# Clustered attention and two feed-forward layers: moving the preparation of a pair of heads within its steps, and rewriting the first head's start

## The chip, the cores and the metric

The kernel runs on one core of one Trainium2 chip. A time is that of one execution on the device in microseconds (us), and smaller is better. The core has five engines with an instruction queue each: TensorE (PE in the profile, with its weight loads apart as PEld), VectorE (DVE), ScalarE (ACT), GpSimd (POOL) and SyncE (SP). SP, and here ACT too, issue DMA transfers. SBUF is the memory on the core; PSUM is the accumulator memory that TensorE writes, in banks.

## The reference

```python
def _attn_ref(q, k, v, centroids):          # 2 batches, 8 heads, 768 rows, 64 wide; 16 centroids a head
    q_n, k_n, c_n = each divided by its norm along the last axis
    q_assign = np.argmax(np.einsum('bhsd,hcd->bhsc', q_n, c_n), axis=-1)
    k_assign = np.argmax(np.einsum('bhsd,hcd->bhsc', k_n, c_n), axis=-1)
    mask = q_assign[:, :, :, None] == k_assign[:, :, None, :]
    scores = np.where(mask, q @ k.T / 8, -1e9)
    return softmax(scores) @ v

x = attention, laid out as 1536 tokens x 512
h = x @ w_in1;  x = softplus(h) @ w_out1                 # 512 -> 2048 -> 512
h = x @ w_in2;  out = (h * clip(h + 3, 0, 6) / 6) @ w_out2
```

A query sees only the keys whose nearest centroid is its own. The matmuls are done on operands split into a rounded part (`hi`) and a rest (`lo`).

## The kernel before

**Stage one, attention.** Two heads form a pair, and there are 8 pairs (two batches of four). A pair takes 12 steps, six blocks of 128 queries for each head, so there are 96 steps. All of stage one is in program order on each engine: the loop at L769 to L792 calls the parts of a step one after the other, for steps -3 to 102, and works several steps ahead. In one turn of the loop these stand: `expo` (ACT, L410: exp with the row sums), `row_max` (DVE, L402: `nm`), `flip` twice (PE transposes `t`, L424; ACT copies them to `pth`, L428; DVE makes the rest `ptl`, L429), `scores` (PE, L394: `s`), `weigh` (PE, L439: `pv`). After every third turn `gather` copies a finished block of `pv` to SBUF (`xs`; ACT, L452 and L454).

**Preparation of a pair.** Between these parts lie seven numbered places, and `at(step, place, function, ...)` hangs a piece of other work there. The table at L515 to L602 does so for the preparation of each later pair. For pair n, with o = 12n - 12: q and k are loaded and split into hi and lo (POOL, L257 to L268; for the first two pairs ACT and DVE); `p_sims` multiplies them by the centroids (PE, `psm`, L294); `p_sims_out` scales that into `sT` (ACT, L300, by `c_r`, one over the centroids' norms); `p_back` transposes it (PE, `pbk`, L307); `p_max` and `p_equal` find the nearest centroid (DVE, `mx` L316 and `eq` L322, both read `pbk` in PSUM); `p_rank` breaks ties (POOL, L329); `p_best` and `p_first` finish the one-hot (DVE, L334 and `oh` L339); `p_onehot` transposes it (PE, `po`, L347); `p_mask` makes the mask rows `mk` (ACT, L353). SP's DMAs then assemble the operands `Q` and `K` from the parts (`assemble`, L371 to L375, and `assemble_mask`, L383).

**One bank for four tiles.** `psm`, `pbk` and `po` of every pair but the first, and `pb`, the transposed row sums of a finished pair (`tot_flip`, PE, L469; ACT copies it to `rT`, L474), come from one pool of PSUM with one buffer:

```python
def bank(n, shape, dt, name):
    if n == 0: ...
    else:
        pl, tag = ps_p, "prep"
```

A tile of it is written only when the last reader of the one before has ended. `tot_flip` of pair n hangs in step 12n + 15, place 0, and that is within the preparation of pair n + 2; it is so for six pairs.

**The start.** SP's queue loads `cT` (the centroids transposed), q and k of the first pair in halves, and `c_sb` (the centroids by rows, four DMAs, L208). A chain of small DVE and ACT operations makes `c_r` of it (L689 to L702, `c_sq` first). The first head's `Q` and `K` come by five DMAs. Then follow the one-hot of the first head, the scores and the loop.

**Stage two, the layers.** 96 steps in a pipeline, each with `h` (PE, L157), the activation `hid_scalar` (for the first layer two softplus on ACT: `g` at L812, `ghi` at L813) and `y` (PE, L845 and L847). The first of them are mixed by the scheduler with the last steps of stage one, as are the conversions of weights (ACT L98 and L122, DVE L106 to L112, POOL or DVE L133, `val`, `pi`, `po`). Softplus and exp lie in different table sets of ScalarE, so a load of the table stands ahead of each change.

Of the kernel before, what the change touches and what calls it, by code (L numbers as in the profile page):

```python
# [8 lines left out]
F32 = mybir.dt.float32  # L9
# [3 lines left out]
AF = mybir.ActivationFunctionType  # L13
# [9 lines left out]
def cluster_attention_then_two_mlps(  # L23
# [13 lines left out]
    nc = tc.nc  # L37
# [17 lines left out]
    def f32(ap):  # L55
        return ap.bitcast(F32)
# [89 lines left out]
    ps_h = []  # L146
    hs = {}

    def phase_a(n, c):
# [11 lines left out]
    def attention():  # L161
        with ExitStack() as st, ExitStack() as st_ld, ExitStack() as st_ps:
# [252 lines left out]
            def flip(t, g):  # L415
                h, jj = t // JH, t % JH
                if jj == 0 and g == 0:
                    st_t[h] = tuple(ptp.tile([P, NJ, HALF], F32R, tag=u, name=u) for u in ("pth", "ptl"))
                pth, ptl = st_t[h]
                pr = st_p[t]  # L420
                pt = ps_t.tile([P, 512], F32, tag="t", name="t")
                for c in range(JH):
                    kt = g * JH + c
                    nc.tensor.transpose(pt[:, c * P:(c + 1) * P], pr[:, kt * P:(kt + 1) * P], ident)  # L424
                src = pt[:, :HALF].rearrange("p (c q) -> p c q", q=P)
                dh = pth[:, g * JH:(g + 1) * JH, jj * P:(jj + 1) * P]
# [88 lines left out]
            for n in range(NP):  # L515
                o = SL * n - SL
                if n > 1:
                    at(max(o + -15, 3), 6, load_qk, n, "q")
                    at(max(o + -11, 4), 6, load_qk, n, "k")
                    at(max(o + -10, 4), 5, p_centroids, n)  # L520
                    q0 = max(o + -11, 7)
                    at(q0, 1, p_split_hi, n, "q", 0)
                    at(q0, 2, p_split_lo, n, "q", 0)
                    at(o + -4, 1, p_split_hi, n, "q", 1)
                    at(o + -4, 2, p_split_lo, n, "q", 1)
                    at(o + -3, 5, p_split_hi, n, "k", 0)
                    at(o + -2, 1, p_split_lo, n, "k", 0)
                    at(o + -1, 1, p_split_hi, n, "k", 1)
                    at(o + -1, 2, p_split_lo, n, "k", 1)
                    at(o + 0, 4, p_sims, n, 0)  # L530
                    at(o + 0, 4, p_sims, n, 1)
                    at(o + 1, 1, p_sims, n, 2)
                    at(o + 1, 4, p_sims, n, 3)
# [4 lines left out]
                    at(o + 3, 4, p_rank, n)  # L538
                    at(o + 4, 6, p_best, n)
                    at(o + 5, 1, p_first, n)  # L540
                    at(o + 6, 4, p_onehot, n)
                    at(o + 6, 6, p_mask, n)
# [4 lines left out]
                    at(o + -3, 6, load_v, n)  # L547
                    at(o + 6, 5, p_values, n, 0)
                    at(o + 7, 4, p_values, n, 1)
                elif n:  # L550
                    at(0, 4, p_centroids, n)
                    at(0, 2, p_split_hi, n, "q", 0)
                    at(0, 2, p_split_lo, n, "q", 0)
                    at(0, 4, p_split_hi, n, "q", 1)
                    at(0, 4, p_split_lo, n, "q", 1)
                    at(1, 2, p_split_hi, n, "k", 0)
                    at(1, 2, p_split_lo, n, "k", 0)
                    at(1, 5, p_split_hi, n, "k", 1)
                    at(1, 5, p_split_lo, n, "k", 1)
                    at(2, 3, p_sims, n, 0)  # L560
                    at(2, 5, p_sims, n, 1)
                    at(3, 3, p_sims, n, 2)
                    at(3, 3, p_sims, n, 3)
                    at(3, 4, p_sims_out, n)
                    at(4, 3, p_back, n)
                    at(4, 6, p_max, n)
                    at(5, 1, p_equal, n)
                    at(5, 1, p_rank, n)
                    at(6, 0, p_best, n)
                    at(6, 0, p_first, n)  # L570
                    at(7, 3, p_onehot, n)
                    at(7, 3, p_mask, n)
                    at(6, 3, assemble, n, 0)
                    at(8, 2, assemble_mask, n, 0)
                    at(11, 3, assemble, n, 1)
                    at(11, 6, assemble_mask, n, 1)
                    at(1, 1, load_v, n)
                    at(7, 0, p_values, n, 0)
                    at(10, 3, p_values, n, 1)
                o += 2 * SL  # L580
                if n < NP - 1:
# [5 lines left out]
                    at(o + 10, 4, fin_scale, n, 1)  # L587
                    at(o + 12, 2, fin_hi, n, 0)
                    at(o + 14, 2, fin_hi, n, 1)
                    at(o + 16, 2, fin_lo, n, 0)  # L590
# [173 lines left out]
            place(1, 0, 1)  # L764
            assemble(0, 1)
            p_values(0, 0)
            fetch_w(0, 0)
# [107 lines left out]
    with tc.manual_schedule():  # L875
# [11 lines left out]
        for n in range(len(steps) + LAG):  # L887
# [18 lines left out]
            if t:  # L906
                hid_scalar(t)
            do(convert_rest, ci, engine=nc.vector)
# [55 lines left out]
```

## Time and profile before

| | us |
|---|---|
| time, median of 3 runs (lowest, highest) | 805.5 (804.8, 806.54) |
| the profiled execution | 804.36 |
| its span | 802.6 |

The mean granted clock is 0.998 in the profiled execution. Busy shares of the span, by engine: PE 96%, DVE 58%, ACT 52%, POOL 19%. The profile shows one execution. The waits list says for each instruction of an engine what ended its idle time; a timeline gives every instruction with its start, its length and, in brackets, the idle time of its engine ahead of it and what ended that; the table of windows gives busy time by engine in a stretch, with the clock that TensorE was granted. Line numbers are those of the kernel before; in the kernel after, the same code stands 3 to 18 lines lower.

### The profile page before, as it was taken

Reading aid. Unit: us, or ns where it says so; the run is one execution under the profiler, and the core shown is the slowest. Engines: PE = TensorE matmul, PEld = TensorE weight load, DVE = VectorE, ACT = ScalarE, POOL = GpSimd, SP = SyncE. Lnnn points to the kernel's source line nnn. Section 1 sums busy time; section 2 is a strip of 40 time slices with the busy share of each in tenths; the row PEclk is TensorE's granted clock in tenths of the full one; section 3 lists DMA queues with packets and bytes.
Section 4 is the critical chain, followed back from the end, with each engine's and each line's share of the span. In section 5 each row is a group of like instructions: output and inputs, shape, how many; then the busy total and the mean of one; then the engine's idle time right before and its main releaser. Section 6 shows DMA issues by size and latency. Waiting matters only on the chain.

```text
span 802.6 us, 10560 instructions
## 1 busy us (share of the span) xinstructions
PE 768.0 (96%) x3835; PEld 643.9 (80%) x3835; DVE 465.0 (58%) x793; ACT 415.8 (52%) x828; POOL 152.2 (19%) x223
## 2 busy tenths in 40 slices
PE   5899898998999899999999999999999999999998
PEld 5788887887878678888888888888888888888886
DVE  5998878778788699942111247779862322232222
ACT  3888788888889856633122234455542222232221
POOL 4466657566333300000000000000000000000000
PEclk9999999999999999999999999999999999999999
DMA  8866455474366092000000156550000100010001
GB/s 210 262 161 164 93 158 134 97 185 94 79 147 228 18 371 104 1 0 1 1 0 1 51 186 205 182 190 27 2 1 0 53 1 0 1 53 0 1 1 52
DMA packets 38180, 70.53 MB, mean 88 GB/s; under 512 B 4432, under 2 KB 22512, under 8 KB 38128
## 3 DMA queue, kind: packets, MB, share of 16 engines
q1 hardware_dynamic: 38128, 69.86, 30.3%
q8 instruction: 30, 0.49, 0.3%
q14 instruction: 22, 0.18, 0.1%
HBM read 46.30 MB, written 3.19 MB: 62 GB/s over the span
## 4 chain that ended last, share of the span: by engine, by line
PE 81%; ACT 6%; DVE 6%; DMA 3%; issue 2%; SPq 1%; ACTq 0%; DVEq 0%
PE h L157 32%; PE y L847 16%; PE y L845 16%; PE s L394 5%; PE t L424 5%; PE pv L439 5%; DMA K<-hik 2%; ACT pth L428 2%; ACT pr L410 2%; PE psm L294 2%; DVE nm L402 1%; DVE ptl L429 1%; SPq L373 1%; ACT mk L353 1%; DMA k<-in_k 0%
## 5 line engine op out<-in xcount | busy, mean ns | idle before, releaser
L157 PE MATMUL h<-xhi,pi 128*128 128x512 f32 x768 | 239.1, 392 | 2.7 <-ACT pr L410 1.5
L157 PEld LDWEIGHTS h<-xhi,pi 128*128 128x128 f32 x768 | 144.0, 188 | 34.4 <-ACT pr L410 1.8
L826 DVE TENSOR_TENSOR glo<-g,ghi 128x512 fp32r<-128x512 f32 x96 | 66.6, 694 | 148.0 <-ACT ghi L813 119.3
L157 PE MATMUL h<-xlo,pi 128*128 128x512 f32 x384 | 150.2, 391 | 0.0
L429 DVE TENSOR_TENSOR ptl<-t,pth 128x384 fp32r<-128x384 f32 x192 | 98.0, 551 | 42.8 <-ACT pth L428 42.8
L845 PE MATMUL y<-ghi,po 128*128 128x512 f32 x384 | 118.9, 391 | 0.2 <-ACT xs L454 0.2
L847 PE MATMUL y<-po,ghi 128*128 128x512 f32 x384 | 118.9, 391 | 0.0
L819 DVE SCALAR_TENSOR_TENSOR g<-u,h 128x512 f32<-128x512 f32 x48 | 33.0, 688 | 127.1 <-ACT u L815 127.1
L815 ACT ACTIVATE u<-h,half 128x512 f32<-128x512 f32 x48 | 33.0, 686 | 128.3 <-PE h L157 128.0
L428 ACT ACTIVATE pth<-t 128x384 fp32r<-128x384 f32 x192 | 84.7, 488 | 26.4 <-PE t L424 25.8
L394 PE MATMUL s<-K,Q 128*128 128x256 f32 (+1 forms) x384 | 90.1, 356 | 4.1 <-ACT pr L410 2.9
L424 PE MATMUL t<-ident,pr 128*128 128x128 f32 x576 | 84.4, 278 | 8.8 <-DVE ptl L429 8.6
L410 ACT ACTIVATE pr<-s,nm 128x768 f32<-128x768 f32 x96 | 86.5, 901 | 9.7 <-DVE nm L402 9.5
L402 DVE TENSOR_REDUCE nm<-s 128x1 f32<-128x768 f32 x96 | 90.6, 945 | 0.5 <-PE s L394 0.5
L812 ACT ACTIVATE g<-h 128x512 f32<-128x512 f32 x48 | 28.5, 594 | 111.1 <-PE h L157 111.1
L424 PEld LDWEIGHTS t<-ident,pr 128*128 128x128 f32 x576 | 66.6, 141 | 23.3 <-DVE ptl L429 20.2
L845 PEld LDWEIGHTS y<-ghi,po 128*128 128x128 f32 x384 | 72.0, 188 | 16.2 <-ACT xs L454 0.7
L157 PEld LDWEIGHTS h<-xlo,pi 128*128 128x128 f32 x384 | 72.2, 188 | 15.7
L847 PEld LDWEIGHTS y<-po,ghi 128*128 128x128 f32 x384 | 72.1, 188 | 15.5
L394 PEld LDWEIGHTS s<-K,Q 128*128 128x128 f32 x384 | 65.6, 189 | 15.0 <-ACT pr L410 5.0
L847 PE MATMUL y<-po,glo 128*128 128x512 f32 x192 | 75.1, 391 | 0.0
L845 PE MATMUL y<-glo,po 128*128 128x512 f32 x192 | 75.0, 390 | 0.0
(124 smaller groups left out, 942.5 us busy)
## 6 DMA issues: line engine op xcount, KB each, us to landing
ri<-in_moe_w_in SPq DMA_DIRECT2D x32, 512.0 KB, 4.6
ro<-in_moe_w_out SPq DMA_DIRECT2D x32, 512.0 KB, 5.3
Q<-hiq SPq DMA_DIRECT2D x16, 384.0 KB, 4.3
K<-hik SPq DMA_DIRECT2D x32, 192.0 KB, 4.6
Q<-loq SPq DMA_DIRECT2D x16, 192.0 KB, 5.4
K<-lok SPq DMA_DIRECT2D x16, 192.0 KB, 4.0
v<-in_v SPq DMA_DIRECT2D x8, 384.0 KB, 3.2
rsb<-row SPq DMA_DIRECT2D x16, 192.0 KB, 4.0
```

The source lines that it names most:

```text
L157: nc.tensor.matmul(hs[n][:, :TB], w[:, c, :], x[c][:, cols], start=(c == 0 and i == 0), stop=(c == NC - 1 and i == 2))
L394: nc.tensor.matmul(ps[:, n0:n1], Q[i][:, u, j * P:(j + 1) * P], K[i][:, u, n0:n1], start=(u == 0), stop=(u == 1),)
L402: nc.vector.tensor_reduce(nm, st_s[t][:, :S], AX.X, ALU.max, negate=True)
L410: nc.scalar.activation(pr, st_s.pop(t)[:, :S], AF.Exp, bias=st_p[t], accum_out=sums_of[n][:, i, j:j + 1])
L424: nc.tensor.transpose(pt[:, c * P:(c + 1) * P], pr[:, kt * P:(kt + 1) * P], ident)
L428: nc.scalar.activation(dh, src, AF.Copy)
L429: nc.vector.tensor_tensor(dl, src, f32(dh), ALU.subtract)
L439: nc.tensor.matmul(st_v[h][:, :HALF], vs[:, kt, i, :], st_t[h][u][:, kt, :], start=(kt == 0 and u == 0), stop=(kt == NJ - 1 and u == 1),)
L815: nc.scalar.activation(t["u"], t["h"], AF.Relu, bias=half, scale=1.0 / 6.0)
L826: nc.vector.tensor_tensor(t["glo"], t["g"], f32(t["ghi"]), ALU.subtract)
L845: nc.tensor.matmul(y[:, :TB], w[:, e, :], x, **fl)
L847: nc.tensor.matmul(y, x[:, e * P:(e + 1) * P], w.rearrange("p c e -> p (c e)"), **fl)
```

## The change

In the table of places, preparation of pairs 2 to 7 is moved: similarities (`psm`, `sT`) one to two steps earlier, `pbk` from place (o+2, 4) to (o+1, 1), `mx` and `eq` from (o+3, 1) and (o+3, 2) to (o+1, 4) and (o+2, 2), `best` and `oh` to places behind `row_max` in two different steps. The splits, loads and centroids that feed these move with them; the second pair's preparation moves one or more steps earlier. The places of `pb` and of `assemble` stay.

At the start ScalarE's queue issues `cT` and `c_sb`; K's split stands behind the centroids' chain; two of the first head's five assembling DMAs stay and the rest is done by copies of POOL and ACT; the clearing of the second head's operands moves behind the first centroids; q and k of the second pair are loaded ahead of v of the first; eight warming transposes stand where 14 did. At the border of the stages, `issue_after` puts the first layer's softplus behind the last `pth`.

```diff
--- before.py
+++ after.py
@@ -145,6 +145,7 @@
     steps = [(l, tb, f) for l in range(2) for tb in range(NB) for f in range(NF)]
     ps_h = []
     hs = {}
+    last_flip = []
 
     def phase_a(n, c):
         layer, tb, f = steps[n]
@@ -200,12 +201,12 @@
 
 
             cT = cb.tile([P, NPAIR, C], F32, name="cT")
-            nc.sync.dma_start(cT, centroids)
+            nc.scalar.dma_start(cT, centroids)
+            c_sb = sm.tile([P, HALF], F32, tag="sT", name="c_sb", bufs=1)[:, :NPAIR * D].rearrange("p (n d) -> p n d", d=D)
+            for r in range(0, P, 2 * C):
+                nc.scalar.dma_start(c_sb[r:r + 2 * C], centroid_rows)
             load_qk(0, "q")
             load_qk(0, "k")
-            c_sb = sm.tile([P, HALF], F32, tag="sT", name="c_sb", bufs=1)[:, :NPAIR * D].rearrange("p (n d) -> p n d", d=D)
-            for r in range(0, P, 2 * C):
-                nc.sync.dma_start(c_sb[r:r + 2 * C], centroid_rows)
 
             Q = [qk.tile([P, 2, S], F32R, name=f"Q{i}") for i in range(2)]
             K = [qk.tile([P, 2, S], F32R, name=f"K{i}") for i in range(2)]
@@ -213,10 +214,12 @@
             cwl = cb.tile([P, 14 * C], F32R, name="cwl")
             nc.gpsimd.memset(f32(cwh), 0.0)
             nc.gpsimd.memset(f32(cwl), 0.0)
-            for i in range(2):
+            def clear(i):
                 o = D * (1 - i)
                 nc.gpsimd.memset(f32(Q[i][o:o + D, 1, :]), 0.0)
                 nc.gpsimd.memset(f32(K[i][o:o + D, 1, :]), 0.0)
+
+            clear(0)
             msc = cb.tile([P, 1], F32, name="msc")
             mbi = cb.tile([P, 1], F32, name="mbi")
             for r in range(0, P, G):
@@ -425,7 +428,7 @@
                 src = pt[:, :HALF].rearrange("p (c q) -> p c q", q=P)
                 dh = pth[:, g * JH:(g + 1) * JH, jj * P:(jj + 1) * P]
                 dl = ptl[:, g * JH:(g + 1) * JH, jj * P:(jj + 1) * P]
-                nc.scalar.activation(dh, src, AF.Copy)
+                last_flip[:] = [nc.scalar.activation(dh, src, AF.Copy)]
                 nc.vector.tensor_tensor(dl, src, f32(dh), ALU.subtract)
 
             def weigh(h, c):
@@ -516,64 +519,62 @@
...
-                    at(o + 1, 6, p_sims_out, n)
-                    at(o + 2, 4, p_back, n)
-                    at(o + 3, 1, p_max, n)
-                    at(o + 3, 2, p_equal, n)
-                    at(o + 4, 6, p_best, n)
-                    at(o + 5, 1, p_first, n)
...
+                    at(o + 0, 4, p_sims_out, n)
+                    at(o + 1, 1, p_back, n)
+                    at(o + 1, 4, p_max, n)
+                    at(o + 2, 2, p_equal, n)
+                    at(o + 4, 2, p_best, n)
+                    at(o + 5, 2, p_first, n)
...
@@ -701,23 +702,38 @@
                 nc.vector.tensor_scalar(c_n, c_n, 1e-6, None, ALU.add)
                 nc.vector.reciprocal(c_r, c_n)
 
+            def assemble_first():
+
+                d = prep[0]
+                (qh, ql), (kh, kl) = d["q"], d["k"]
+                lo_rows, hi_rows = slice(0, D), slice(D, P)
+                nc.gpsimd.tensor_copy(Q[0][lo_rows], qh[lo_rows].unsqueeze(1).to_broadcast([D, 2, S]))
+                nc.sync.dma_start(f32(Q[0])[hi_rows, 0], f32(ql)[lo_rows])
+                nc.sync.dma_start(f32(K[0])[hi_rows, 0], f32(kh)[lo_rows])
+                nc.scalar.activation(K[0][lo_rows, 0], kh[lo_rows], AF.Copy)
+                nc.gpsimd.tensor_copy(K[0][lo_rows, 1], kl[lo_rows])
+
             p_centroids(0)
-            for nm in "qk":
-                for hf in range(2):
-                    p_split_hi(0, nm, hf)
-                    p_split_lo(0, nm, hf)
+            clear(1)
+            p_split_hi(0, "q", 0)
+            p_split_lo(0, "q", 0)
+            p_split_hi(0, "q", 1)
+            p_split_lo(0, "q", 1)
             for step in range(3):
                 c_root(step)
             c_unit()
-            assemble(0, 0)
-            load_v(0)
+            for hf in range(2):
+                p_split_hi(0, "k", hf)
+                p_split_lo(0, "k", hf)
+            assemble_first()
+            load_qk(1, "q")
+            load_qk(1, "k")
             for c in (0, 2, 1, 3):
                 p_sims(0, c)
-            load_qk(1, "q")
-            load_qk(1, "k")
             p_sims_out(0)
             p_back(0)
-            for _ in range(14):
+            load_v(0)
+            for _ in range(8):
                 nc.tensor.transpose(warm[:, :P], ident, ident)
 
             oh = sm.tile(full, BF16, tag="oh", name="oh", bufs=1)
@@ -763,6 +779,8 @@
             scores(0)
             place(1, 0, 1)
             assemble(0, 1)
+            p_split_hi(1, "q", 0)
+            p_split_hi(1, "q", 1)
             p_values(0, 0)
             fetch_w(0, 0)
             p_values(0, 1)
@@ -904,7 +922,9 @@
             do(convert_bits, co, 0)
             do(convert_bits, co, 1)
             if t:
-                hid_scalar(t)
+
+                with tc.issue_after(last_flip[0].ins):
+                    hid_scalar(t)
             do(convert_rest, ci, engine=nc.vector)
             do(convert_abs, ni)
             if t:
```

PE, at the preparation of the third pair, before. `pb` is the tile of the pair finished last.

```order
L424 MATMUL t<-ident,pr 128x128 x6
L307 MATMUL pbk<-ident,sT 128x128 x3
L394 MATMUL s<-K_160,Q_158 128x512 x2
L394 MATMUL s<-K_160,Q_158 128x256 x2
L439 MATMUL pv<-pth,vs 128x384
L439 MATMUL pv<-ptl,vs 128x384
L439 MATMUL pv<-pth,vs 128x384
L439 MATMUL pv<-ptl,vs 128x384
L469 MATMUL pb<-ident,rs 12x128
L424 MATMUL t<-ident,pr 128x128 x6
```

PE, the same place, after; four rows of `pv` and then `pb` follow.

```order
L442 MATMUL pv<-ptl,vs 128x384
L310 MATMUL pbk<-ident,sT 128x128 x3
L427 MATMUL t<-ident,pr 128x128 x6
L397 MATMUL s<-K_160,Q_158 128x512 x2
L397 MATMUL s<-K_160,Q_158 128x256 x2
L442 MATMUL pv<-pth,vs 128x384
L442 MATMUL pv<-ptl,vs 128x384
L442 MATMUL pv<-pth,vs 128x384
L442 MATMUL pv<-ptl,vs 128x384
L427 MATMUL t<-ident,pr 128x128 x6
L397 MATMUL s<-K_160,Q_158 128x512 x2
L397 MATMUL s<-K_160,Q_158 128x256 x2
```

Between `pbk` and `pb` there was one `s` and one block of `pv`; now there are two of each and two `t`.

DVE, from `mx` of the same pair on, before.

```order
L316 TENSOR_REDUCE mx<-pbk 128x24
L402 TENSOR_REDUCE nm<-s 128x1
L322 TENSOR_TENSOR eq<-pbk,mx 128x384
L429 TENSOR_TENSOR ptl<-t,pth 128x3x128 x2
L402 TENSOR_REDUCE nm<-s 128x1
L429 TENSOR_TENSOR ptl<-t,pth 128x3x128 x2
L334 TENSOR_REDUCE mx_973<-eq 128x24
L339 TENSOR_TENSOR oh<-eq,mx_973 128x384
L402 TENSOR_REDUCE nm<-s 128x1
L429 TENSOR_TENSOR ptl<-t,pth 128x3x128 x2
```

DVE, the same place, after.

```order
L319 TENSOR_REDUCE mx<-pbk 128x24
L405 TENSOR_REDUCE nm<-s 128x1
L325 TENSOR_TENSOR eq<-pbk,mx 128x384
L432 TENSOR_TENSOR ptl<-t,pth 128x3x128 x2
L405 TENSOR_REDUCE nm<-s 128x1
L432 TENSOR_TENSOR ptl<-t,pth 128x3x128 x2
L405 TENSOR_REDUCE nm<-s 128x1
L337 TENSOR_REDUCE mx_943<-eq 128x24
L432 TENSOR_TENSOR ptl<-t,pth 128x3x128 x2
L405 TENSOR_REDUCE nm<-s 128x1
L342 TENSOR_TENSOR oh<-eq,mx_943 128x384
L432 TENSOR_TENSOR ptl<-t,pth 128x3x128 x2
```

`mx` and `eq` keep their order among their neighbours (they move up by a step as a group), and `best` and `oh`, which stood together ahead of one `nm`, each stand behind an `nm`.

ACT at the border of the stages, before.

```order
L812 ACT_TABLE_LOAD
L812 ACTIVATE g<-h 128x512
L428 ACTIVATE pth<-t 128x3x128 x2
L410 ACT_TABLE_LOAD
L410 ACTIVATE pr,sums<-s,nm 128x768
L428 ACTIVATE pth<-t 128x3x128
L122 ACTIVATE pi_3669<-val 128x512
L813 ACT_TABLE_LOAD
L813 ACTIVATE ghi<-h 128x512
L428 ACTIVATE pth<-t 128x3x128
```

ACT at the same place, after.

```order
L431 ACTIVATE pth<-t 128x3x128 x2
L413 ACTIVATE pr,sums<-s,nm 128x768
L431 ACTIVATE pth<-t 128x3x128
L122 ACTIVATE pi_3663<-val 128x512
L431 ACTIVATE pth<-t 128x3x128
L98 ACTIVATE val<-ro_528 128x512
L431 ACTIVATE pth<-t 128x3x128 x2
L830 ACT_TABLE_LOAD
L830 ACTIVATE g<-h 128x512
```

Of three loads of the table one is left, behind the last `pth`.

## Rows read from the trace of the kernel before

**Rows 1.** Waits of PE, whole span: us in total, times, longest us.

```profile
PE pb L469 <- DVE eq L322: 8.8, 6, 1.5
```

**Rows 2.** Windows: us, busy us (instructions) of PE, PEld, DVE, ACT, POOL, PEclk, DMA, GB/s.

```profile
16.00:46.00 30.00, 24.88 (x156) 20.87 (x157) 28.38 (x48) 25.41 (x56) 17.67 (x27) 1.00 0.81 238
...
154.84:185.66 30.82, 28.90 (x188) 25.67 (x189) 24.70 (x42) 25.96 (x59) 20.10 (x28) 1.00 0.55 135
...
266.00:269.00 3.00, 2.39 (x7) 1.99 (x8) 0.56 (x1) 2.97 (x6) 1.46 (x2) 0.53 0.00 0
...
290.00:320.00 30.00, 30.00 (x131) 24.38 (x130) 29.59 (x54) 18.27 (x35) 0.00 (x0) 1.00 0.57 216
```

**Rows 3.** Timeline, 184 to 188 us: start, us, operation, [idle before, releaser].

```profile
184.96 0.55 DVE L322 TENSOR_TENSOR eq<-pbk,mx 128x384 f32<-128x384 f32 x1
...
185.66 0.27 PE L469 MATMUL pb<-ident,rs 128*12 128x128 f32 x1 [1.47 <-DVE eq L322]
...
186.29 0.88 ACT L428 ACTIVATE pth<-t 128x384 fp32r<-128x384 f32 x2 [1.09 <-PE t L424]
...
186.81 1.02 DVE L429 TENSOR_TENSOR ptl<-t,pth 128x384 fp32r<-128x384 f32 x2 [1.30 <-ACT pth L428]
```

**Rows 4.** Timeline, 160 to 162 us, `best` and `oh` of the preparation.

```profile
161.51 1.01 PE L424 MATMUL t<-ident,pr 128*128 128x128 f32 x6 [0.25 <-DVE ptl L429]
```

**Rows 5.** Lines by form of DVE, 46 to 234 us: busy, mean ns | idle before.

```profile
L429 DVE TENSOR_TENSOR ptl<-t,pth 128x384 fp32r<-128x384 f32 x146 | 74.5, 551 | 35.8 <-ACT pth L428 35.7
...
L339 DVE TENSOR_TENSOR oh<-eq,mx 128x384 bf16<-128x384 f32 x6 | 5.7, 955 | 0.2
```

**Rows 6.** Timeline, 261 to 290 us, the border of the stages.

```profile
261.60 1.28 ACT L812 ACT_TABLE_LOAD   x1
...
262.89 0.60 ACT L812 ACTIVATE g<-h 128x512 f32<-128x512 f32 x1
...
263.91 1.02 DVE L429 TENSOR_TENSOR ptl<-t,pth 128x384 fp32r<-128x384 f32 x2 [1.60 <-ACT pth L428]
...
264.52 0.55 PE L424 MATMUL t<-ident,pr 128*128 128x128 f32 x3 [1.90 <-DVE ptl L429]
...
266.61 1.22 PE L157 MATMUL h<-xhi,pi 128*128 128x512 f32 x2 [1.55 <-ACT pr L410]
...
266.98 0.56 DVE L429 TENSOR_TENSOR ptl<-t,pth 128x384 fp32r<-128x384 f32 x1 [1.45 <-ACT pth L428]
...
269.40 0.92 DVE L826 TENSOR_TENSOR glo<-g,ghi 128x512 fp32r<-128x512 f32 x1 [1.87 <-ACT ghi L813]
```

**Rows 7.** Timeline, 275 to 280 us: the same DVE operation twice, and POOL.

```profile
275.89 0.68 DVE L108 SCALAR_TENSOR_TENSOR val<-ri,val 128x512 uint32<-128x512 uint32 x1
...
277.42 1.37 POOL L133 TENSOR_TENSOR po<-val,po 128x512 fp32r<-128x512 f32 x1 [6.29 <-ACT po L122]
...
277.67 1.67 DVE L108 SCALAR_TENSOR_TENSOR val<-ro,val 128x512 uint32<-128x512 uint32 x1
```

**Rows 8.** Timeline, 0 to 16 us, the start.

```profile
3.62 1.02 ACT L254 ACTIVATE hiq<-q 128x384 fp32r<-128x384 f32 x2 [1.61 <-DMA q<-in_q]
...
7.12 0.56 DVE L268 TENSOR_TENSOR lok<-k,hik 128x384 fp32r<-128x384 f32 x1 [0.22 <-ACT hik L254]
...
7.59 0.42 DVE L689 TENSOR_TENSOR c_sq<-c_sb 128x256 f32<-128x256 f32 x1
...
8.33 0.33 PE L294 MATMUL psm<-hik,cwl 128*128 128x384 f32 x1
...
11.00 0.18 DVE L702 RECIPROCAL c_r<-c_n 128x4 f32<-128x4 f32 x1
...
11.26 0.58 ACT L300 ACTIVATE sT<-psm,c_r 128x384 f32<-128x384 f32 x1 [2.12 <-DVE c_r L702]
...
14.61 0.50 POOL L363 CAST vs<-v 128x384 fp32r<-128x384 f32 x1 [8.46 <-DMA v<-in_v]
```

**Rows 9.** DMA issues, 0 to 20 us: KB each, median us to landing.

```profile
c_sb<-in_centroid_rows SPq DMA_DIRECT2D x4, 32.0 KB, 3.3
```

More of the change, by code (lines that the diff above doesn't have):

```diff
@@ L518, in attention @@
                     at(max(o + -15, 3), 6, load_qk, n, "q")
-                    at(max(o + -11, 4), 6, load_qk, n, "k")
-                    at(max(o + -10, 4), 5, p_centroids, n)
-                    q0 = max(o + -11, 7)
+                    at(max(o + -13, 4), 6, load_qk, n, "k")
+                    at(max(o + -9, 4), 5, p_centroids, n)
+                    q0 = max(o + -11, 6)
                     at(q0, 1, p_split_hi, n, "q", 0)
                     at(q0, 2, p_split_lo, n, "q", 0)
[L524 to L533, printed above, removed]
-                    at(o + 1, 6, p_sims_out, n)
-                    at(o + 2, 4, p_back, n)
-                    at(o + 3, 1, p_max, n)
-                    at(o + 3, 2, p_equal, n)
-                    at(o + 3, 4, p_rank, n)
-                    at(o + 4, 6, p_best, n)
-                    at(o + 5, 1, p_first, n)
-                    at(o + 6, 4, p_onehot, n)
+                    at(o + -5, 1, p_split_hi, n, "q", 1)
+                    at(o + -5, 2, p_split_lo, n, "q", 1)
+                    at(o + -4, 1, p_split_hi, n, "k", 0)
+                    at(o + -4, 2, p_split_lo, n, "k", 0)
+                    at(o + -3, 5, p_split_hi, n, "k", 1)
+                    at(o + -2, 1, p_split_lo, n, "k", 1)
+                    at(o + -1, 4, p_sims, n, 0)
+                    at(o + -1, 4, p_sims, n, 1)
+                    at(o + 0, 1, p_sims, n, 2)
+                    at(o + 0, 4, p_sims, n, 3)
+                    at(o + 0, 4, p_sims_out, n)
+                    at(o + 1, 1, p_back, n)
+                    at(o + 1, 4, p_max, n)
+                    at(o + 2, 2, p_equal, n)
+                    at(o + 2, 4, p_rank, n)
+                    at(o + 4, 2, p_best, n)
+                    at(o + 5, 2, p_first, n)
+                    at(o + 6, 3, p_onehot, n)
                     at(o + 6, 6, p_mask, n)
@@ L547, in attention @@
                     at(o + -3, 6, load_v, n)
-                    at(o + 6, 5, p_values, n, 0)
-                    at(o + 7, 4, p_values, n, 1)
+                    at(o + 5, 5, p_values, n, 0)
+                    at(o + 6, 4, p_values, n, 1)
                 elif n:
[L551 to L576, printed above, removed]
+                    at(-2, 2, p_split_lo, n, "q", 0)
@@ new lines, in attention @@
+                    at(-1, 2, p_split_lo, n, "q", 1)
+                    at(-1, 1, p_centroids, n)
+                    at(-1, 1, p_split_hi, n, "k", 0)
+                    at(-1, 1, p_split_lo, n, "k", 0)
+                    at(0, 1, p_split_hi, n, "k", 1)
+                    at(0, 1, p_split_lo, n, "k", 1)
+                    at(1, 3, p_sims, n, 0)
+                    at(1, 3, p_sims, n, 2)
+                    at(1, 5, p_sims, n, 1)
+                    at(1, 5, p_sims, n, 3)
+                    at(2, 1, p_sims_out, n)
@@ new lines, in attention @@
+                    at(2, 3, p_back, n)
+                    at(2, 6, p_max, n)
+                    at(3, 2, p_equal, n)
+                    at(3, 4, p_rank, n)
+                    at(4, 2, p_best, n)
+                    at(5, 2, p_first, n)
+                    at(6, 3, p_onehot, n)
+                    at(6, 6, p_mask, n)
+                    at(5, 3, assemble, n, 0)
+                    at(7, 1, assemble_mask, n, 0)
+                    at(10, 5, assemble, n, 1)
+                    at(11, 4, assemble_mask, n, 1)
@@ L587, in attention @@
                     at(o + 10, 4, fin_scale, n, 1)
-                    at(o + 12, 2, fin_hi, n, 0)
-                    at(o + 14, 2, fin_hi, n, 1)
+                    at(o + 12, 5, fin_hi, n, 0)
+                    at(o + 14, 5, fin_hi, n, 1)
                     at(o + 16, 2, fin_lo, n, 0)
```

## The prediction

> **What bounds the kernel now.** I read the waits of TensorE first, since it is busy for 96% of the span: what shortens the kernel is either its idle time or work that it no longer does, and the change takes no work from it after the start. The largest single entry is `pb` behind DVE's `eq`: six times, 1.47 us each, 8.8 us in all [rows 1]. Then I read the windows. A pair in the middle lasts 30.82 us, of which PE is busy for 28.90, ACT for 25.96 and DVE for 24.70; so PE is idle for 1.92 us in a pair, and no other engine is full [rows 2]. In 16 to 46 us, by contrast, DVE is busy for 28.38 of 30 us and PE for 24.88: there DVE sets the pace [rows 2]. The timeline of one `pb` shows the mechanism: `eq` ends at 185.51, `pb` starts at 185.66 after 1.47 idle, the two steps of `t` stand behind it in PE's order, and then ACT (`pth`) has waited 1.09 and DVE (`ptl`) 1.30 [rows 3]. Nothing `pb` computes is late; it is the bank that is still being read. The border of the stages is the second place: two of the three table loads delay ACT, PE idles 1.90 and 1.55, and the granted clock falls to 0.53 over 266 to 269 us, so mostly at the lower level, after that idle time [rows 2, 6].
>
> **The sum goes against the profiled execution**, 804.36 us, 802.6 of it span; the median of the runs is 805.5, that is 1.1 above it, and differences carry over.
>
> **Pairs 2 to 7: the bank.** What is moved is the same work, so no cost is added on any engine. Before, `mx`, `nm` and `eq` stand between `pbk` and `pb` with only one `s` and one block of `pv` on PE's side; after, PE has a further `t`, `s` and `pv` in between, and DVE has done a whole `ptl` behind `eq`. A step gives PE about 30.82 / 12 = 2.57 us, more than the 1.47 that is missing, so the bank should be free. The next reader that may be late, `po`, comes only in step o + 6. So 6 x 1.47 = 8.8 goes. Beside that `best` and `oh` no longer stand together ahead of one `nm`; the `t` behind them idled 0.25 [rows 4], and I take half of it, 6 x 0.125 = 0.75, as DVE now has `oh` ahead of `ptl` instead. Together -9.5. The lower bound is what ACT can hand on: it waited 1.09 in that step, and if its `xs` copies are late next, only 6 x 1.09 = 6.5 comes back [rows 3]. The upper bound is all of PE's idle time in a pair, 6 x 1.92 = 11.5 [rows 2]. Moves that I cost at nothing: splits, centroids and loads run one to two steps earlier on POOL (20.10 busy of 30.82) [rows 2] and SP, whose waiting DMAs stand in the same order; and `assemble` keeps its places.
>
> **The border.** `g` and `ghi` behind the last `pth` leave one load of the table of three: 2 x 1.28 = 2.56 less on ACT [rows 6], the lower bound. The value is PE's two waits that hang on these loads, 1.90 + 1.55 = 3.45, less nothing for the first softplus coming later, since 290 to 320 us has PE full [rows 2] and its `y` follows with slack. DVE waited 1.60, 1.45 and 1.87 in the same stretch, 4.92 [rows 6]: the upper bound, because DVE, busy for 29.59 of 30 us behind the border [rows 2], does the conversions that PE takes next. I take -3.45 and add nothing for the clock.
>
> The Trainium skill, "ScalarE: Activation LUTs", section "What ACT_TABLE_LOAD costs", puts about 1.28 us on a load and 1.38 us on a drain with it, 2.66 in all. The load agrees; of a drain the trace shows nothing, for the load ends at 262.88 and `g` starts at 262.89 [rows 6]. By the page two switches less would be worth an estimated 5.3 us instead of 2.56.
>
> **The start.** Before: `c_sq` at 7.59, `c_r` done at 11.18, 3.59 later, and `sT` at 11.26, which waited for `c_r` alone; K's split (`lok`, ended 7.68) was ahead of the chain, and the similarities ended at 8.66 [rows 8]. After: the fourth `c_sb` transfer waits on ScalarE's queue for the first half of q, which had landed by 3.62 [rows 8]; with 3.3 us to landing [rows 9] it is there at about 6.9 (estimated), 0.7 earlier. Chain to 10.5, then two `lok` of 0.56 to 11.6, and of the similarities the last two products behind them, about 0.6 by 2 x 0.33: `sT` at 12.2 instead of 11.26, +0.9. ACT's five issues stand ahead of `hiq`, but `hiq` is no longer last. The lower bound is -0.7, if K's split isn't what ends last and the earlier landing counts in full. The upper bound is set by the copies on POOL. Nothing of before copies 1536 elements a row; the nearest is a cast of 384 in 0.50 [rows 8], so Q's copy is some 2.0, and were it to hold DVE's chain up throughout, the start is +2.9. Gains behind `sT` (fewer DMAs on SP, the second pair's q and k earlier) I put at nothing: 16 to 46 us is bound by DVE, which does the same work [rows 2]; +-1.
>
> Sum: -9.5 - 3.45 + 0.9 = -12.0: 792.3 for the profiled execution, 793.5 against the median.
>
> **Rivals.**
> *DVE held by POOL at the start.* The two do meet in this kernel: `val` on DVE took 1.67 beside POOL's `po` of 1.37, and 0.68 alone; it ended 0.55 after POOL did [rows 7]. So it looks as if it waited for all of it. With Q's copy of 2.0 inside the chain: -12.0 + 2.0 = -10.0, 795.5. Against it: the chain's operations are small, and the copy may end before them.
> The Trainium skill, "SBUF — State Buffer", section "SBUF: two separate sides", says so as a rule: the port pair of VectorE and GpSimd is an exclusive lock, and an operation of DVE with two SBUF inputs blocks fully while GpSimd has it. By that rule, the rows agree.
>
> *Only what ACT had free comes back.* -6.5 - 2.56 + 0.9 = -8.2: 797.3. For it: ACT is the busiest after PE in a pair [rows 2]; against it: DVE idles 35.8 us behind `pth` in 188 [rows 5], so the chain has slack.
>
> *The bank isn't free in time*, since `eq` moved with `mx` and there may be something else late (`sT`, `pbk`): then -3.45 + 0.9 = -2.6, 802.9. Against it the rows between `pbk` and `pb`.
>
> *Slower: DVE's four preparation operations show in full.* Each now stands behind an `nm` and ahead of the `ptl` that the next `t` waits for. `mx`, `eq` and `best` take 0.55 each, as `eq` does [rows 3], `oh` 0.955 in the mean, since POOL often runs beside it [rows 5]: 2.6 a pair. If no slack passes from step to step, a pair gains 1.47 and pays 2.6: 6 x 1.13 = +6.8, with border and start +4.2: 809.7. It decides against the change from (8.8 + 3.45 - 0.9) / 6 = 1.9 us a pair. Against it: before, the same operations stood in the same chain, and `best` with `oh` together cost PE 0.25 [rows 4].
>
> **Chances.** Forecast 0.74; POOL against DVE 0.11; ACT's slack only 0.07; bank not free 0.04; slower 0.04. What one can tell from no change here is about 0.2%, 1.6 us, so 803.9 is the border: the bank's case lies on it and is split in halves. Faster 0.94, same 0.02, slower 0.04. Range: the least of the known terms, -6.5 - 2.56 + 2.9 = -6.2, gives 799.3; the most, -11.5 - 4.92 - 0.7 = -17.1, gives 788.4; with the first pair's +-1 I set 788 to 800.
>
> **What would show it.** Right: the waits list without `pb` behind `eq` and no new entry above 0.5 us a pair; a pair of about 29.2 us; one table load at the border, no waits of 1.90 and 1.55, and a granted clock near 1 over that stretch; `sT` at about 12.2. Wrong: the pair still over 30, with `t` behind `ptl` or `s` behind `pr` grown (ACT's or DVE's case); `c_sq` or the chain's two-input operations stretched beside POOL (the port); a transfer of the masks that PE waits for, as SP's queue is fuller in other steps.

## The result and the profile after

| | before | after |
|---|---|---|
| median (lowest to highest), us | 805.15 (804.4 to 806.54) | 794.62 (793.61 to 795.4) |
| runs | 4 | 4 |
| ratio, 95% interval | | 0.9867 (0.9849 to 0.9884) |
| profiled execution; its span | 804.36; 802.6 | 795.4; 793.6 |

The kernel became 10.5 us faster; 793.5 was predicted. The profiled spans differ by 9.0. That the time came out near the forecast is partly luck: two terms were wrong in opposite directions. One instruction, `pb`, stands once in every pair and cuts the span into the same stages in both kernels. Its start in us (the first two, then the sixth to the eighth), before:

```profile
61.09 0.27 PE L469 MATMUL pb<-ident,rs 128*12 128x128 f32 x1 [1.47 <-DVE eq L322]
...
217.07 0.27 PE L469 MATMUL pb<-ident,rs 128*12 128x128 f32 x1 [1.47 <-DVE eq L322]
245.49 0.27 PE L469 MATMUL pb<-ident,rs 128*12 128x128 f32 x1
276.25 0.27 PE L469 MATMUL pb<-ident,rs 128*12 128x128 f32 x1
```

And after, the same landmarks:

```profile
65.83 0.27 PE L472 MATMUL pb<-ident,rs 128*12 128x128 f32 x1
...
212.15 0.27 PE L472 MATMUL pb<-ident,rs 128*12 128x128 f32 x1
240.13 0.27 PE L472 MATMUL pb<-ident,rs 128*12 128x128 f32 x1
265.81 0.27 PE L472 MATMUL pb<-ident,rs 128*12 128x128 f32 x1
```

No `pb` waits now. The differences, stage by stage, with the 1.47 wait ahead of the first `pb` counted to the pairs:

| stage | before | after | difference | predicted |
|---|---|---|---|---|
| start, to the first `pb` without its wait | 59.62 | 65.83 | +6.2 | +0.9 |
| first to sixth `pb`, and the first one's wait | 155.98 + 1.47 | 146.32 | -11.1 | } -9.5 |
| sixth to seventh | 28.42 | 27.98 | -0.4 | } |
| seventh to eighth (the border) | 30.76 | 25.68 | -5.1 | } -3.45 |
| behind the eighth, to the end of the span | 526.35 | 527.79 | +1.4 | } |
| sum | 802.6 | 793.6 | -9.0 | -12.0 |

**The pairs.** A window from one `pb` to the next in the middle, after (us, busy us of PE, PEld, DVE, ACT, POOL), and what PE waited for in it:

```profile
153.59:182.87 29.28, 29.07 (x188) 25.54 (x187) 24.40 (x43) 25.90 (x60) 20.14 (x28) 1.00 0.59 142
```

```profile
PE s L397 <- ACT pr L413: 0.2, 1, 0.2
```

PE is now busy for 29.07 of 29.28 us, against 28.90 of 30.82 [rows 2]; one short wait is left. The rest of that pair's gain, beyond 1.47, is small. But the pair I had read was a short one: the five intervals of before are 30.92, 31.40, 31.43, 30.82 and 31.41, and 31.20 in the mean. In the three long ones POOL's `vs` began some 0.3 us ahead of `oh`, and `oh` took 1.13 to 1.15. Before, DVE and POOL in the pair I had read, and then in a long one:

```profile
159.57 0.56 DVE L339 TENSOR_TENSOR oh<-eq,mx 128x384 bf16<-128x384 f32 x1
159.59 1.41 POOL L364 TENSOR_TENSOR vs<-v,vs 128x384 fp32r<-128x384 f32 x1
...
190.10 1.00 POOL L364 TENSOR_TENSOR vs<-v,vs 128x384 fp32r<-128x384 f32 x1
190.38 1.14 DVE L339 TENSOR_TENSOR oh<-eq,mx 128x384 bf16<-128x384 f32 x1
```

In the first `oh` began 0.02 ahead, took 0.56, and POOL took 1.41 instead of 1.00; in the second it began 0.28 after POOL and took 1.14. Its mean was 955 ns [rows 5]. After, the mean is 592 ns (lines by form, 46 to 234 us):

```profile
L342 DVE TENSOR_TENSOR oh<-eq,mx 128x384 bf16<-128x384 f32 x6 | 3.6, 592 | 0.0
```

**The border** went as the rows said. One load of the table, behind the last `pth`, ACT after:

```profile
261.19 0.85 ACT L431 ACTIVATE pth<-t 128x384 fp32r<-128x384 f32 x2
262.06 1.28 ACT L830 ACT_TABLE_LOAD   x1
263.35 0.60 ACT L830 ACTIVATE g<-h 128x512 f32<-128x512 f32 x1
```

PE's waits of 1.90 and 1.55 [rows 6] are gone, and the granted clock is 1.00 over 262 to 270 us. Of the 5.1 us, 1.4 are given back behind it; some 1.0 of that is a second wait of PE for the conversion `pi` of DVE. PE's waits from 255 us on, before and after:

```profile
PE h L157 <- DVE pi L133: 1.2, 1, 1.2
...
PE h L158 <- DVE pi L133: 2.2, 2, 1.1
```

**The start** is where I was wrong. Timeline of after, with what I had put elsewhere:

```profile
6.50 1.46 POOL L710 CAST Q<-hiq 64x1536 fp32r<-64x1536 f32 x1
6.57 1.67 DVE L690 TENSOR_TENSOR c_sq<-c_sb 128x256 f32<-128x256 f32 x1 [1.18 <-DMA c_sb<-in_centroid_rows]
...
8.93 0.20 ACT L693 ACTIVATE c_n<-c_n 128x4 f32<-128x4 f32 x1 [4.24 <-DVE c_n L692]
9.17 0.21 ACT L694 ACTIVATE c_n<-c_n 128x4 f32<-128x4 f32 x1
9.28 0.92 ACT L257 ACTIVATE hik<-k 128x384 fp32r<-128x384 f32 x2
...
9.84 0.44 PE L297 MATMUL psm<-hik,cwh 128*128 128x384 f32 x1 [2.40 <-ACT hik L257]
...
11.33 1.01 DVE L271 TENSOR_TENSOR lok<-k,hik 128x384 fp32r<-128x384 f32 x2
...
11.92 0.69 PE L297 MATMUL psm<-lok,cwh 128*128 128x384 f32 x1 [1.64 <-DVE lok L271]
...
13.37 0.52 PE L297 MATMUL psm<-hik,cwl 128*128 128x384 f32 x1
...
13.93 0.58 ACT L303 ACTIVATE sT<-psm,c_r 128x384 f32<-128x384 f32 x1 [2.85 <-PE psm L297]
```

`sT` starts at 13.93, 2.7 later than before [rows 8]. Three things add up. The first: `c_sq` takes 1.67 beside POOL's copy (+1.25). The second: `lok` stands on DVE behind the whole chain and starts at 11.33. The third: PE then runs at the lower level: a product takes 0.52 instead of 0.33 [rows 8], and behind the first `lok` there are five of them, not two. `hik` stands late too, on ACT behind the two `c_n` of the chain, and PE idles 2.40 for it; but it ended at 10.20, over 1 us ahead of `lok`, so it isn't what made `sT` late. Windows, after:

```profile
7.00:10.00 3.00, 0.60 (x3) 0.16 (x1) 2.34 (x6) 1.03 (x4) 0.96 (x1) 1.00 0.17 35
...
12.00:15.00 3.00, 2.33 (x7) 1.82 (x8) 0.54 (x2) 0.58 (x1) 0.82 (x1) 0.50 0.88 209
```

The granted clock was 1.00 in 7 to 10 us, while PE was busy for 0.60 of 3 us, and 0.50 in 12 to 15 us. Over 12 to 28 us its mean is 0.61; in the profile of before it is 1.00. The other 3.5 of the 6.2 us are lost between `sT` and the first `pb`. One part of them stands in the timeline of DVE, which is busy for 4.00 of 4 us in 20 to 24: `loq` of the second pair, the rest of q, which now meets POOL's `vs`. The change loads v of the first pair later, and the first `vs` begins at 19.95 instead of 14.61 [rows 8].

```profile
20.53 0.99 POOL L367 TENSOR_TENSOR vs<-v,vs 128x384 fp32r<-128x384 f32 x1
20.78 1.16 DVE L268 SCALAR_TENSOR_TENSOR loq<-q,hiq 128x384 fp32r<-128x384 f32 x1
...
22.73 1.07 DVE L268 SCALAR_TENSOR_TENSOR loq<-q,hiq 128x384 fp32r<-128x384 f32 x1
```

The first experiment below has the same tables and the start of before; there the two take 0.55 and 0.54, 1.1 us less in all.

### The profile page after: what moved, and what is told of

Same layout as the page of the kernel before. It is cut to its first block, busy times and chain, and to the rows that moved or that the text cites. A ratio compares the mean times of both kernels' runs of the same rounds, so it can differ in the third digit from the quotient of the medians.

```text
span 793.6 us, 10533 instructions
## 1 busy us (share of the span) xinstructions
PE 772.8 (97%) x3829; PEld 645.7 (81%) x3829; DVE 462.1 (58%) x793; ACT 413.8 (52%) x827; POOL 155.0 (20%) x225
## 4 chain that ended last, share of the span: by engine, by line
PE 85%; ACT 5%; DVE 4%; DMA 3%; issue 1%; POOL 1%; SPq 0%; ACTq 0%; DVEq 0%; POOLq 0%
PE h L158 32%; PE y L865 17%; PE y L863 16%; PE s L397 6%; PE t L427 6%; PE pv L442 6%; PE psm L297 2%; ACT pr L413 2%; DMA Q<-hiq 1%; ACT pth L431 1%; DMA K<-hik 1%; ACT mk L356 1%; DVE val L108 1%; ACT xs L455 0%; ACT xs L457 0%
## 5 line engine op out<-in xcount | busy, mean ns | idle before, releaser
L397 PE MATMUL s<-K,Q 128*128 128x256 f32 (+1 forms) x384 | 91.8, 361 | 4.5 <-ACT pr L413 3.2
L427 PE MATMUL t<-ident,pr 128*128 128x128 f32 x576 | 88.4, 282 | 2.1 <-DVE ptl L432 1.4
```

The costliest lines, as they stand in the source:

```text
L397: nc.tensor.matmul(ps[:, n0:n1], Q[i][:, u, j * P:(j + 1) * P], K[i][:, u, n0:n1], start=(u == 0), stop=(u == 1),)
```

## The experiments

Each was timed against the kernel before on the same chip; the ratio's interval follows, and "below before" is the difference of the two medians there.

**The start of before in the changed kernel.** Edit:

```diff
-            nc.scalar.dma_start(cT, centroids)
+            nc.sync.dma_start(cT, centroids)
...
-                nc.scalar.dma_start(c_sb[r:r + 2 * C], centroid_rows)
+                nc.sync.dma_start(c_sb[r:r + 2 * C], centroid_rows)
...
+            for nm in "qk":
+                for hf in range(2):
+                    p_split_hi(0, nm, hf)
+                    p_split_lo(0, nm, hf)
             for step in range(3):
                 c_root(step)
             c_unit()
-            for hf in range(2):
-                p_split_hi(0, "k", hf)
-                p_split_lo(0, "k", hf)
-            assemble_first()
+            assemble(0, 0)
```

> The changed kernel with the start of before (centroids by SP's queue, K's split ahead of the centroids' chain, five assembling DMAs, no copies on POOL). Theory A, the start was made slower by the change: the first pb was 4.7 us later than before although a wait of 1.47 ahead of it had gone, so some 6 us come back, 788 to 790 us, and sT stands near 11.3 us with a granted clock of 1 over 12 to 28 us. Rival B, most of the delay comes from the second pair's earlier preparation, which this kernel keeps: then less than 2 us come back, 793 us or more, and the first pb stays later than 64 us.

791.72 us, 0.9817 (0.9796 to 0.9837). The profile (789.63) is theory A to the letter: the first `pb` is 5.5 us earlier, and all behind it lasts as in the changed kernel (200.0 us to the eighth `pb`):

```profile
11.00 0.58 ACT L304 ACTIVATE sT<-psm,c_r 128x384 f32<-128x384 f32 x1 [2.12 <-DVE c_r L704]
...
17.33 0.55 DVE L269 SCALAR_TENSOR_TENSOR loq<-q,hiq 128x384 fp32r<-128x384 f32 x1
...
18.67 0.54 DVE L269 SCALAR_TENSOR_TENSOR loq<-q,hiq 128x384 fp32r<-128x384 f32 x1
...
60.29 0.27 PE L473 MATMUL pb<-ident,rs 128*12 128x128 f32 x1
```

The median is between the theories: its runs lie from 789.63 to 793.73, wider than those of the changed kernel, and the profile is of the shortest. The two shortest have a mean granted clock of 1.00, the other three 0.995 to 0.997.

**The table of pairs 2 to 7 alone, on the kernel before.** Edit, the whole block `if n > 1:` and the places of `fin_hi`, of which three lines stand here:

```diff
-                    at(o + 2, 4, p_back, n)
-                    at(o + 3, 1, p_max, n)
-                    at(o + 3, 2, p_equal, n)
...
+                    at(o + 1, 1, p_back, n)
+                    at(o + 1, 4, p_max, n)
+                    at(o + 2, 2, p_equal, n)
```

> The kernel before with the new table for pairs 2 to 7 alone (and the two places of the finishing split on POOL that moved). Theory A, the table alone carries what the pairs gained: the six intervals give 1.47 + 9.66 us and the next 0.4, so about 11.5 us off the 805.2 of before, 793.5 to 794.5, pb without a wait and a pair of 29.3 us. Rival B, part of the shorter pair comes from elsewhere (the later start leaves the splits more time): then 796 to 800 us, with waits of pb, sT or the splits left.

794.1 us, 0.9852 (0.9832 to 0.9872), 11.7 less than before: theory A. No `pb` waits, the first three stand 29.20 and 29.25 apart, and the mean of `oh` is 596 ns.

**The border alone, on the kernel before.** Edit:

```diff
-                hid_scalar(t)
+                with tc.issue_after(last_flip[0].ins):
+                    hid_scalar(t)
```

> The kernel before with the first softplus held behind the last pth, nothing else. Theory A: last pb 5.1 us earlier and 1.4 us given back behind it to the conversions on DVE, so 3.6 us less, about 801.5 us, one table load and a granted clock of 1 over the border. Rival B: the border pays only when attention ends as it does in the changed kernel; then under 2 us, 803.2 or more.

801.5 us, 0.994 (0.9923 to 0.9957), 4.4 less: theory A. The seventh and the eighth `pb` stand 25.68 apart, as in the changed kernel. The waits of `pb` are those of before:

```profile
PE pb L470 <- DVE eq L323: 8.8, 6, 1.5
```

**`best` and `oh` back at their places, in the changed kernel.** Edit:

```diff
-                    at(o + 4, 2, p_best, n)
-                    at(o + 5, 2, p_first, n)
+                    at(o + 4, 6, p_best, n)
+                    at(o + 5, 1, p_first, n)
```

> The changed kernel with best and oh put back to their places of before, both ahead of one nm; the bank's part stays. Theory A, the pairs gained 1.9 us and not 1.5 since oh no longer meets POOL (its mean went from 955 to 592 ns) and no longer stands with best: then 0.2 to 0.5 us a pair come back, +1.5 to +3 us, 796 to 797.5 us. Rival B, the bank alone gave the whole of it: no difference within 0.8 us, 794 to 795.4.

798.01 us, 0.99 (0.9884 to 0.9915): 7.8 below before, where the changed kernel is 10.5 below, so 2.7 come back; the plain medians differ by 3.4, a little above theory A's range. Rival B is out. From the first to the seventh `pb` the profile takes 178.3 us instead of 174.3, 4.0 more; its start was 1.3 shorter, with `c_sq` at 0.43, which the edit doesn't touch. What came back is a longer `oh` and the `t` behind it, which idles 0.25 as before [rows 4]:

```profile
L342 DVE TENSOR_TENSOR oh<-eq,mx 128x384 bf16<-128x384 f32 x6 | 4.7, 782 | 0.2
```

```profile
131.61 0.55 PE L427 MATMUL t<-ident,pr 128*128 128x128 f32 x3 [0.25 <-DVE ptl L432]
```

So of the pairs' 11.6 us some 8 are the bank and 3 to 4 the places of `best` and `oh`.

**K's split ahead of the centroids' chain, in the changed kernel.** Edit:

```diff
+            for hf in range(2):
+                p_split_hi(0, "k", hf)
+                p_split_lo(0, "k", hf)
             for step in range(3):
                 c_root(step)
             c_unit()
-            for hf in range(2):
-                p_split_hi(0, "k", hf)
-                p_split_lo(0, "k", hf)
             assemble_first()
```

> The changed kernel with K's split (ACT and DVE) ahead of the centroids' chain again, the rest of its start unchanged. Theory A, the order of K's split is the larger part of the delayed start: PE then has K's products at about 6 to 8 us and waits for c_r alone, sT starts at 11.4 to 11.8 instead of 13.93, and the first pb comes 3 to 5 us earlier, if the lower granted clock over 12 to 28 us goes with it; 790 to 792 us. Rival B, the delay is the copies on POOL against DVE: then sT gains under 1 us and the time stays at 793.5 or more.

791.86 us, 0.9821 (0.9807 to 0.9834), 14.3 below before, where the changed kernel is 10.5 below: theory A in time. But `sT` starts at 12.31, not at 11.4 to 11.8, because POOL's copy now meets `lok`:

```profile
6.37 2.30 DVE L271 TENSOR_TENSOR lok<-k,hik 128x384 fp32r<-128x384 f32 x2 [1.18 <-ACT hik L257]
6.80 1.46 POOL L710 CAST Q<-hiq 64x1536 fp32r<-64x1536 f32 x1
```

**Q's copy by DMA instead of POOL, in the changed kernel.** Edit:

```diff
-                nc.gpsimd.tensor_copy(Q[0][lo_rows], qh[lo_rows].unsqueeze(1).to_broadcast([D, 2, S]))
+                nc.sync.dma_start(f32(Q[0])[lo_rows], f32(qh)[lo_rows].unsqueeze(1).to_broadcast([D, 2, S]))
```

> The changed kernel with Q's copy of the first head on SP's DMA queue instead of POOL. Theory A: c_sq takes 0.42 us again instead of 1.67, so the chain and K's split behind it move 1.25 earlier, sT to 12.7, and the time falls by 1 to 1.5 us; the idle time of PE ahead of K's products remains and the granted clock over 12 to 28 us stays low. Rival B, POOL against DVE is the larger part: sT below 12 and 3 us or more.

792.84 us, 0.9832 (0.9818 to 0.9845), 13.3 below before. `c_sq` takes 0.42, `sT` starts at 12.11 and the first `pb` at 63.74, 2.1 earlier. So the time lies between the theories; the clock over 12 to 28 us stayed low:

```profile
12.00:28.00 16.00, 12.97 (x57) 10.35 (x57) 11.90 (x21) 7.79 (x17) 6.46 (x10) 0.60 0.79 216
```

**Transposes in PE's first idle time, in the changed kernel.** Edit:

```diff
-            for c in (0, 2, 1, 3):
+            for c in (0, 2):
+                p_sims(0, c)
+            for _ in range(20):
+                nc.tensor.transpose(warm[:, :P], ident, ident)
+            for c in (1, 3):
                 p_sims(0, c)
```

> The changed kernel with 20 more warming transposes on PE between the products of Q and those of K, where PE idled 2.4 us; nothing waits for them. If the lower granted clock after that idle time is itself a cost: clock near 1 over 12 to 28 us, sT about 0.6 earlier (five products at 0.34 instead of 0.52), the first pb 2 to 3 us earlier, 792 to 793 us. Rival: the clock costs nothing as DVE and ACT bound the start; first pb and time within 0.8 us.

792.64 us, 0.9838 (0.9815 to 0.9862), with runs from 791.15 to 796.8. It can't be read as meant: the profile (796.8) has the clock at 0.59 over 12 to 28 us and the first `pb` at 67.27, later than without the fill. But it shows something else, `c_sq` undisturbed beside the same copy, and the chain's third operation stretched in its place:

```profile
6.47 0.42 DVE L690 TENSOR_TENSOR c_sq<-c_sb 128x256 f32<-128x256 f32 x1 [1.07 <-DMA c_sb<-in_centroid_rows]
6.52 1.70 POOL L710 CAST Q<-hiq 64x1536 fp32r<-64x1536 f32 x1
...
7.38 0.86 DVE L692 TENSOR_SCALAR c_n<-c_ss 128x4 f32<-128x4 f32 x1
```

Here DVE began 0.05 ahead and POOL took 1.70; in the profile of after POOL began 0.07 ahead with 1.46, and DVE took 1.67. The one that starts later waits. `c_n`, 0.17 alone, started later too: it ended at 8.24, 0.02 after the copy. So here the chain still lost 0.7.

**Transposes in all three idle times.** Edit, beside the one before (8 more stand ahead of `p_sims_out(0)`):

```diff
                     nc.tensor.matmul(ps[:, :HALF], w, x, start=(m == 0), stop=(m == 11))
+                    if n == 0 and m == 3:
+                        for _ in range(14):
+                            nc.tensor.transpose(warm[:, :P], ident, ident)
```

> The changed kernel with warming transposes in all three idle times of PE at the start: 20 ahead of K's products, 14 between the first of them and the next, 8 ahead of pbk. Theory A, the clock falls since PE idles there, and the low clock is a cost of its own beside the waits: clock near 1 over 12 to 28 us, first pb 1.5 to 3 us earlier than in the changed kernel, 791.5 to 793 us. Rival B, the clock falls anyway, or DVE and ACT set the pace of that stretch: the time within 0.8 us of the changed kernel's 794.6.

792.18 us, 0.9832 (0.9818 to 0.9846): theory A's time. But its profile mixes two gains: `c_sq` was undisturbed there too (0.42, and `c_n` 0.86), and the clock rose to 0.79 over 12 to 28 us only, with 0.50 in 20 to 24. What the clock alone costs is not told apart by it.

**Both repairs of the start, without and with 20 transposes ahead of `pbk`.** The edits are those of K's split and of Q's copy together, and for the second run:

```diff
+            for _ in range(20):
+                nc.tensor.transpose(warm[:, :P], ident, ident)
             p_sims_out(0)
```

> The changed kernel with both repairs of its start: K's split ahead of the centroids' chain, and Q's copy by SP's DMA instead of POOL. Theory A, these two are what delayed it: lok is not stretched (0.5 each), c_sq starts near 7.4, sT at about 11, the first pb at 60 to 61.5, 790 to 792 us, no slower than with the whole start of before. Rival B, something else in the new start costs too (two instead of five assembling DMAs with copies, six warming transposes fewer, the centroids' queue): sT at 11 but the first s later than 16, 792.5 us or more.

> As the run with both repairs, plus 20 warming transposes on PE while it waits for the first sT. If the lower clock after that wait is a cost there: clock 1 over 12 to 28 us and 0.8 to 2 us less than without them. If not: the same within 0.8 us.

792.12 us, 0.9826 (0.9812 to 0.984), and 791.15 us, 0.9823 (0.9809 to 0.9836). `sT` is at 10.91 in the first, as theory A has it, and the time is just outside its range; but the first `s` whose masks are there comes at 16.15, 0.2 later than before, and the first `pb` at 63.51, which is rival B's sign without its 792.5. Against the run with the start of before, `sT` is as early and the first `pb` 3.2 later: the two `loq` take 1.03 and 1.07 beside `vs` here too, 1.0 of it, and the granted clock is 0.50 over 24 to 28 us. The two repairs do not add. The fill's 1 us lies within the intervals, and with it the clock over 12 to 28 us was 0.79 against 0.71, not 1.

**The start of before with 24 transposes ahead of the first `pbk`.** Edit, on the first kernel of this section:

```diff
+            for _ in range(24):
+                nc.tensor.transpose(warm[:, :P], ident, ident)
             p_sims_out(0)
```

> The new tables and the border with the start of before, plus 24 warming transposes on PE where it waits 3 us for the first sT. Theory: that idle time is at the edge of a lower clock, which fell in one profile (0.89 over 12 to 28 us with the first pb 1.6 us later) and not in another of the same start; with the fill the clock stays at 1 in all executions, the time is 788 to 790.5 us, and its runs lie closer together than 789.6 to 793.7. Rival: the spread has another cause; median as without the fill, 791 to 792.5, and the same spread.

791.72 us, 0.9829 (0.9812 to 0.9846), the median without the fill, and the same spread, 789.85 to 794.37: the theory fell. In the profiles of both, the shortest executions, the clock is 1.00 over 12 to 28 us; the two longest of this one have a mean of 0.995, with the fill in place.

**Two parts of the change alone, on the kernel before.** The edits are those of the table of pairs 2 to 7 and of the border; start and the second pair's table are those of before.

> The kernel before with two parts of the change alone: the table for pairs 2 to 7 and the first softplus behind the last pth; the start and the second pair's table are those of before. Theory A, the two parts add: 11.7 + 4.4 us were measured apart, so 789 to 790.5 us, 1 to 2 us less than with the second pair's new table on the start of before (791.7), whose part is then a small loss. Rival B, the table of the second pair gains or costs nothing and the parts overlap: 791.2 to 792.5.

788.57 us, 0.9797 (0.9778 to 0.9815): the fastest of all, a little under theory A's range and 17.1 less than before, where the two parts apart gave 11.7 and 4.4. It beats the changed kernel clear of both intervals. So what the change did to the start and to the second pair costs 17.1 - 10.5 = 6.6 us, about the +6.2 of the landmarks:

```profile
59.28 0.27 PE L470 MATMUL pb<-ident,rs 128*12 128x128 f32 x1
```

## Why the prediction was right, and where it was not

The direction and the time's range held, and the pairs were the largest term; the sum was -12.0, and the profiles gave -9.0, the medians -10.5. That the sum was no further off is luck: the pairs gave 2.1 more than forecast and the start took 5.3 more. The start, put at the smallest term, was the second largest.

*Pairs, -9.5; measured -11.6 by landmarks and -11.7 alone on the kernel before.* The mechanism was right: the bank's waits of 8.8 are gone, and no new entry of that size stands in the list. The term for `best` and `oh` was mis-sized, 0.75 instead of some 3: it was worked out from one 0.25 us wait in a pair in which `oh` had started ahead of POOL. The row that had the size was there, `oh` with a mean of 955 ns where an undisturbed one takes 0.56; I used it for the slower rival, as a price, and did not ask whether the move would end it.

*Border, -3.45; measured -3.6 by landmarks, -4.4 alone.* Right, with its bounds: 5.1 came at the border and 1.4 went again behind it.

*Start, +0.9; measured +6.2.* This step failed: "Chain to 10.5, then two `lok` of 0.56 to 11.6, and of the similarities the last two products behind them". `sT` came at 13.93, not 12.2. The chain ended at 11.41, since the rival of DVE held by POOL came true within it: `c_sq` lost 1.25, not the 2.0 of its price, and the copy of 1536 took 1.46 instead of the 2.0 estimated from 384 elements. The two `lok` took about the time forecast. Behind them 1.6 us passed instead of 0.6: PE takes its products in order, five stood behind the first `lok`, and at the lower level they followed each other at 0.32 us, so the last two weren't free to start when the second `lok` was there. And I put what lies behind `sT` at nothing with +-1, since DVE "does the same work" there. It does, but the work took longer: the two `loq` lost 1.1 beside POOL. In all, that stretch cost 3.5 in the profile, with the granted clock at 0.61 over 12 to 28 us.

*The rivals.* ACT's slack, the bank still taken and DVE's operations in full are out: no `pb` waits. The slower rival's reason held in reverse, since `oh` became shorter.

Open: how the 3.5 us behind `sT` divide. The 1.1 of `loq` are read from the traces, and no run moves the load of v alone; the rest lies in a stretch with the lower clock. What the clock costs by itself two profiles of one and the same start show: from `sT` to the first `pb` the run of the border alone takes 1.9 more than the kernel before, with a granted clock of 0.89 over 12 to 28 us against 1.00. But two runs with the same start and the same clock of 1.00, that of the table alone and that of the two parts, differ by 0.8 there. So the new table of the second pair isn't shown to cost anything: with the start of before the first `pb` comes at 60.29 with it, and without it at 59.28 in one profile and at 60.28 in the other:

```profile
60.28 0.27 PE L469 MATMUL pb<-ident,rs 128*12 128x128 f32 x1
```

By medians it costs 3.0, each against the kernel before on its chip, with intervals that overlap. Why the runs with that start and the new table spread over 4 us stays open too. The longer ones mostly show a lower granted clock, but idle time ahead of `pbk` isn't the reason, for the fill didn't change it, and no profile of a longer one is there to say where the clock fell.

## What to carry to other kernels

Where an instruction of one queue moves behind a chain, write down what stands ahead of it on its engine, and on the engine that takes its results count everything that is queued behind the first of them, not the last alone. Where a load moves, ask which engines will then work side by side. Read a repeated stage at all its repeats before taking its size, since one repeat may be the one without a collision. And take a change of several parts apart: here two parts gave 17 us, and the other two took more than 6 of them back.

## What the runs showed of the hardware

Which of DVE and POOL starts first decides who waits. Three profiles show the same pair of operations: POOL ahead by 0.07 us made DVE's 0.42 into 1.67; DVE ahead by 0.05 and by 0.02 left it at 0.42 and made POOL's 1.46 into 1.70 and 1.72, the latter in the run with all three fills:

```profile
6.49 0.42 DVE L693 TENSOR_TENSOR c_sq<-c_sb 128x256 f32<-128x256 f32 x1 [1.09 <-DMA c_sb<-in_centroid_rows]
6.51 1.72 POOL L713 CAST Q<-hiq 64x1536 fp32r<-64x1536 f32 x1
```

The Trainium skill, "SBUF — State Buffer", section "SBUF: two separate sides", says that of an operation of DVE with two SBUF inputs and one of GpSimd that reads SBUF, whichever starts first has the shared port pair for the whole instruction and that the other fully blocks. The runs agree in who waits, on both sides of it, and so do `oh` and `vs` in the profile of before, 0.02 and 0.28 us apart. `c_sq` is released by the landing of `c_sb`, so a landing that differs by a tenth of a microsecond decides which of the two waits. It doesn't decide the whole delay: with DVE ahead the later `c_n` took 0.86 instead of 0.17, and the chain's first three operations ended at 8.24 us, against 8.90 with POOL ahead and 7.50 in the run that has the copy done by DMA.

In the changed kernel the granted clock fell to 0.50 behind a stretch in which PE was mostly idle (0.60 busy of 3 us, clock 1.00 at the time). In the profile of before PE also idled 3.23 us ahead of `pbk`, and the clock stayed at 1.00; in that of the border alone, with 2.98 idle at the same place, it fell to 0.50 in 12 to 14 us and the first `pb` came 1.6 later. So the fall is not settled by that idle time alone.
